# Attention, an MLP and a mixture of experts in one kernel: the next stage's first operands loaded and split elsewhere in attention's last iterations

## The chip, the cores and the metric

The kernel runs on one core of a Trainium2 chip. The core has a matmul engine (TensorE, PE in the profile, with its weight loads as PEld), a vector engine (VectorE, DVE), a scalar engine (ScalarE, ACT), GpSimd (POOL) and SyncE (SP), which here does nothing but issue DMAs. The profile counts 16 DMA engines that carry what SP and POOL issue. Each compute engine works its own instructions in order and waits at semaphores for the others. The metric is the device time in microseconds of one execution.

## The reference, cut to what matters

Three stages follow each other; all is float32.

```python
# attention, for B = 8 batches and H = 8 heads, S = 512 tokens, 32 state rows, D = 64
a     = softmax(x @ state.T * scale);   xread = a  @ state     # tokens read the state
a2    = softmax(state @ x.T * scale);   sread = a2 @ x         # the state reads the tokens
x     = concat([xread, sread]) -> rows of B*(512+32) tokens x 512
# an MLP over all 4352 rows
h = x @ w_in;  g = h - tanh(h);  x = g @ w_out
# one of 8 experts for each row
out[row] = gate[row] * (relu(x[row] @ w1[e]) @ w2[e])
```

## The kernel before

**Attention** (lines 418 to 759) takes 16 units, a unit being four heads of one batch: unit i is batch i // 2, half i % 2. A hand-written loop over t (line 704, t = 1 to 18) runs them as a pipeline: iteration t turns the tokens of unit t (`attn_x`), has the scores and both softmaxes of unit t-1, the reads of unit t-2, and in `attn_read_turn` turns the state's result xs of unit t-3 into xo, which goes to the scratch tensor `x_state_t` in DRAM. Beside it the loop makes sixteen pieces of state @ w_in (`sw_part`, t = 1 to 16), which go to the scratch tensor `state_w_in`, and the tokens' probabilities of each unit go to `probs_t`. The matmul that would form xread is not made: the next stage multiplies the probabilities with state @ w_in instead.

Stores are collected in `later`, and `flush` at the head of the next iteration issues them, each time as state_w_in, x_state_t, state_w_in, probs_t. Loads are issued in the iterations too: `attn_load` the tokens xc of unit t+1 (five buffers), `win_load` a piece of w_in. SP works this list strictly in order. Its DMAs use eight counters in turn, so that an issue also waits until the eighth one before it has landed.

**The MLP** (lines 780 to 1113) goes over steps i = 16 b + f, with batch b and slice f of the hidden width. `mm1(b, f)` is six matmuls hp from the split operands at (the probabilities, as ath and atl) and sw (state @ w_in, as swh and swl). Each operand is a sum of a rounded high part (ACT's copy) and a low part (DVE's subtraction), both made by `split` (line 363). `g_series` turns hp into g on ACT and DVE, `g_split` splits g (low part on POOL for b = 0), `mm2` multiplies with w_out. For b = 0 the parts of w_out are still being made: `dec_load` loads the raw words, `dec_bits` joins them on ACT and DVE, `dec_split` writes them into the tile w1t.

The first batch's operands are fetched inside attention's loop: `load_sw(0, 0)` (two loads, one for each four heads) and `load_at(0)` read the scratch tensors into the raw tiles swf and atf, which have one buffer each; `split_sw` and `split_at` split a half at a time. These calls are what the change moves. The load of swf for four heads is

```python
t = raw["sw"] = pm.tile([P, 2, NX], F32, tag="swf", name="swf", bufs=1)
for c in range(2):
    nc.sync.dma_start(t[:, c], swd[q, b // 4, 4 * c : 4 * c + 4, b % 4])
```

so its source is four blocks (heads) of 32 rows of 2 KB. The tile xo has two buffers: `tmp("xo", (P, 2, NS))`, and the third xo in a row waits until the first has been stored.

The order on PE, ACT, DVE and SP is that of the code in attention's loop; around the boundary to the MLP each engine follows its own list, shown below where it differs.

Of the kernel before, what the change touches and what calls it, by code (L numbers as in the profile page):

```python
# [57 lines left out]
def whole(  # L58
# [102 lines left out]
    class Decoder:  # L161
# [32 lines left out]
        def split(self, key, hi, lo):  # L194
            m = self.parts.pop(key)
            return [nc.scalar.copy(hi, m), rest(nc.gpsimd, lo, m, hi)]
# [170 lines left out]
    def load_at(b):  # L367
        if b < B:
            t, src = pm.tile([P, 2, S], F32, tag="atf", name="atf", bufs=1), atd[b]
        else:  # L370
            t, src = pm.tile([P, NPR, NW], F32, tag="atf", name="xsf", bufs=1), xsd
        raw["at"] = t
        nc.sync.dma_start(t, src)

    def split_at(b, half):
        t = raw["at"]
        if half == 0:
            shape = list(t.shape)
            at[b] = tuple(
                pw.tile(shape, F32R, tag=n, name=n, bufs=2) for n in ("ath", "atl")  # L380
            )
        n = t.shape[1] // 2
        c = slice(half * n, half * n + n)
        split(at[b][0][:, c], at[b][1][:, c], t[:, c])

    def load_sw(b, q):
        t = raw["sw"] = pm.tile([P, 2, NX], F32, tag="swf", name="swf", bufs=1)
        for c in range(2):
            nc.sync.dma_start(
                t[:, c],  # L390
                swd[q, b // 4, 4 * c : 4 * c + 4, b % 4],
            )

    def split_sw(b, q, c):
        if c == 0:
            sw[b, q] = tuple(
                pw.tile([P, 2, NX], F32R, tag=n, name=n, bufs=2) for n in ("swh", "swl")
            )
        h, l = sw[b, q]
        split(h[:, c], l[:, c], raw["sw"][:, c])  # L400
# [12 lines left out]
    def dec_bits(b, f):  # L413
        dec.absolute((b, f))
        dec.bits((b, f))


    with ExitStack() as pe:
# [4 lines left out]
        def tmp(name, shape=(P, R, P), dt=F32, bufs=2):  # L423
            return pa.tile(list(shape), dt, tag=name, name=name, bufs=bufs)
# [38 lines left out]
        def load_state():  # L463
            nc.sync.dma_start(
                z[:, 1 : G + 1], state.rearrange("b h n d -> (b h n) d").rearrange("(p g) d -> p g d", g=G)
            )
# [4 lines left out]
        def turn_state(o, j0):  # L471

            n = min(4, G // 2 + o - j0)
            pt = ps_m.tile([P, 4, P], F32, tag="m", name="pt_state")
            for j in range(n):
                g = 1 + 2 * (j0 + j) - o
                nc.tensor.transpose(pt[:, j, :], z[:, g : g + 2].rearrange("p g d -> p (g d)"), ident)
            for up in range(2):
                js = [j for j in range(n) if 0 <= 2 * (j0 + j) - o + up < G]
                if not js:  # L480
                    continue
                g = 2 * (j0 + js[0]) - o + up
                rows = slice(up * D, up * D + D)
                for m in range(NS // G):
                    dst = st_g[rows, :, :, m, g : g + 2 * len(js) - 1 : 2]
                    src = pt[rows, js[0] : js[-1] + 1].rearrange(
                        "p j (b h m) -> p h b m j", b=B, h=H
                    )[:, :, :, m]
                    (nc.vector.tensor_copy if up else nc.scalar.copy)(dst, src)

        def split_state(k):
            c = slice(2 * k, 2 * k + 2)
            nc.scalar.copy(sth[:, c], st[:, c])
            rest(nc.vector, stl[:, c], st[:, c], sth[:, c])
# [5 lines left out]
        def win_load(i):  # L500
            n, k = divmod(i, NPR)
            wdec.load(i, wi32[k * P : (k + 1) * P, 2 * n * NX : 2 * (n + 1) * NX])

        def win_split(i):
            win[i] = tmp("winh", (P, NX), F32R, 3), tmp("winl", (P, NX), F32R, 3)
            wdec.split(i, *win[i])
# [28 lines left out]
        def attn_load(i):  # L535
            b, c = units[i]
            xcs[i] = tmp("xc", (P, 4, R, D), F32, 5)
            nc.sync.dma_start(
                xcs[i], x[b, 4 * c : 4 * c + 4].rearrange("h (p r) d -> p h r d", r=R)
            )  # L540
# [119 lines left out]
        def attn_read_turn(i):  # L660
            b, c = units[i]
            pt = ps_m.tile([P, P], F32, tag="m", name="pt_r")
            nc.tensor.transpose(pt, xss.pop(i).rearrange("p o d -> p (o d)"), ident)
            pt = pt.rearrange("p (k h n) -> p k h n", h=2, n=NS)
            xo = tmp("xo", (P, 2, NS))
            for hh in range(2):
                rows = slice(hh * D, (hh + 1) * D)
                nc.vector.tensor_copy(xo[rows], pt[rows, :, hh])
            later.append((xsd[:, 2 * c : 2 * c + 2, b * NS : (b + 1) * NS], xo))

        NU = len(units)
        LEAD = 3

        def piece(t):

            return [when.index(t)] if t in when else []
# [3 lines left out]
        with tc.manual_schedule():  # L680
            load_state()
            for i in piece(1):
                win_load(i)
            attn_load(0)
            for i in piece(2):
                win_load(i)
            attn_load(1)
            for o, j in ((0, 0), (0, 4), (1, 0), (1, 4), (1, 8)):
                turn_state(o, j)
            attn_x(0)  # L690
            for i in piece(1):
                wdec.absolute(i)
                wdec.bits(i)
            split_state(0)
            for i in piece(1):
                win_split(i)
            for i in piece(3):
                win_load(i)
            for k in range(1, NPR):
                split_state(k)  # L700
            for i in piece(2):
                wdec.absolute(i)
                wdec.bits(i)
            for t in range(1, NU + LEAD):
                def at_(fn, lag, *args):
                    if 0 <= t - lag < NU:
                        fn(t - lag, *args)

                now = piece(t)
                flush()  # L710
                at_(attn_load, -1)
                for i in piece(t + 3):
                    win_load(i)
                at_(attn_scores, 1)
                at_(attn_state, 1)
                at_(attn_x, 0)
                at_(attn_turn, 2)
                for i in now:
                    sw_part(i, 0)
                for i in piece(t + 2):  # L720
                    wdec.absolute(i)
                at_(attn_read_turn, 3)
                at_(attn_turn_scores, 1)
                at_(attn_state_exp, 1)
                at_(attn_soft, 1)
                for i in piece(t + 1):
                    win_split(i)
                for i in now:
                    sw_part(i, 1)
                at_(attn_soft_exp, 1)  # L730
                at_(attn_probs, 2)
                at_(attn_read, 2)
                at_(attn_state_norm, 1)
                at_(attn_read_copy, 2)
                for i in piece(t + 2):
                    wdec.bits(i)
                at_(attn_norm, 1)
                if t == NU - 1:
                    load_sw(0, 0)
                    load_at(0)  # L740
                    for f in range(3):
                        dec_load(0, f)
                if t == NU:
                    split_sw(0, 0, 0)
                    split_at(0, 0)
                if t == NU + 1:
                    split_sw(0, 0, 1)
                    split_at(0, 1)
                    dec_bits(0, 0)
                    load_sw(0, 1)  # L750
                if t == 1:
                    nc.sync.dma_start(lists.rearrange("(p n) t -> p n t", p=P), unlisted)
                    nc.sync.dma_start(yd[NTOK : NTOK + 1], zero[0:1])
                    for b in range(B):
                        nc.sync.dma_start(
                            yd[b * SEQ + S : (b + 1) * SEQ],
                            zero[b % 4 * NS : (b % 4 + 1) * NS],
                        )
            flush()
# [20 lines left out]
    with ExitStack() as pe:  # L780
# [294 lines left out]
        with tc.manual_schedule(engines={EN.PE, EN.Activation, EN.DVE, EN.SP}):  # L1075
# [71 lines left out]
            at_ = along(ij[:, 0:E], rank, ALU.is_equal)  # L1147
            nbp = small("nbp", E)
            wzp, cep = (const.tile([P, E], F32, name=n) for n in ("wzp", "cep"))
            for n, (dst, src) in enumerate(((nbp, nb), (wzp, wz))):  # L1150
                t = square()
# [315 lines left out]
    with tc.manual_schedule(engines={EN.PE, EN.SP, EN.Activation, EN.DVE}):  # L1467
# [26 lines left out]
        t = keep("t", NSB)  # L1494
# [71 lines left out]
    n = nc.values_load(used[0:1, 0:1], min_val=NBLK, max_val=NSB)  # L1566
# [35 lines left out]
```

## Time and profile before

| | us |
|---|---|
| three runs | 1287.59, 1290.66, 1291.16 |
| their median | 1290.66 |
| the profiled execution | 1288.32 |
| its span, first to last instruction | 1286.1 |
| PE busy in the span | 1233.2 (96%) |
| attention | to about 127 |
| MLP | from about 130 to 782 |
| experts | the rest |

The profiled execution's own time is 2.2 us above its span. The times of the change's place are read as instants from the start of the span. In the timeline a row has the start, the duration of the group, the engine and line, and in brackets the idle time ahead of it with what ended it. Rows of SP (SPq) show when a DMA was issued, not when it landed.

### The profile page before, as it was taken

The numbers are of one execution on the slowest core, as the hardware profiler recorded it, in microseconds if no ns is written. First come the engines' busy times: TensorE is split into PE (matmuls) and PEld (weight loads), VectorE is DVE, ScalarE is ACT, GpSimd is POOL, SyncE is SP. The second block draws the span as 40 slices with busy tenths as digits, with TensorE's granted clock in tenths as the row PEclk, the third lists the DMA queues.
The fourth block names the chain that finished last, engine by engine and source line by source line (L and its number), as shares of the span: only waits on it lengthen the run. The fifth ranks groups of instructions, "written<-read, shape, count | busy, mean of one in ns | idle before, by whom it ended". The sixth has DMA issues, their size and how long they took to land. (4 is left out here: it accounts for less than half of the span.)

```text
span 1286.1 us, 22737 instructions
## 1 busy us (share of the span) xinstructions
PE 1233.2 (96%) x6759; PEld 974.1 (76%) x6759; DVE 887.3 (69%) x1515; ACT 857.3 (67%) x1587; POOL 276.6 (22%) x315
## 2 busy tenths in 40 slices
PE   7989788999999999999999999999999999999994
PEld 4555566777777878777787888788888888888883
DVE  7998899677666767576666557566767767576562
ACT  7988677767676767667676673566665657566551
POOL 3333355112010101001010122323232222221100
PEclk8999799999999999999999999999999999999997
DMA  8998642413222222312232471755587877735251
GB/s 263 335 344 276 204 145 82 147 57 125 83 98 72 77 75 57 113 57 93 82 97 85 134 255 40 247 172 174 199 319 266 281 258 260 283 128 193 75 194 35
DMA packets 90277, 208.33 MB, mean 162 GB/s; under 512 B 14162, under 2 KB 30549, under 8 KB 88354
## 3 DMA queue, kind: packets, MB, share of 16 engines
q1 hardware_dynamic: 75682, 162.33, 38.0%
q0 software_dynamic: 14464, 44.40, 9.8%
q8 instruction: 64, 1.05, 0.4%
q14 instruction: 67, 0.55, 0.2%
HBM read 315.42 MB, written 75.03 MB: 304 GB/s over the span
## 5 line engine op out<-in xcount | busy, mean ns | idle before, releaser
L209 DVE SCALAR_TENSOR_TENSOR gs<-gs,gu 128x512 f32<-128x512 f32 (+1 forms) x144 | 104.0, 722 | 180.1 <-ACT gs L207 180.0
L859 PE MATMUL y<-w1t,gl 128*128 128x512 f32 x544 | 217.4, 400 | 8.6 <-POOL gl L159 8.0
L859 PE MATMUL y<-w1t,gh 128*128 128x512 f32 x544 | 223.2, 410 | 1.6 <-ACT gh L848 1.6
L859 PE MATMUL y<-w,gh 128*128 128x512 f32 x544 | 214.9, 395 | 0.0
L1450 PE MATMUL o<-w2t,w 128*128 (+1 forms) x888 | 212.8, 395 | 1.4 <-DVE w2t L1367 1.2
L1423 PE MATMUL h<-w1t,w 128*128 (+1 forms) x888 | 212.3, 395 | 0.0
L1367 DVE TENSOR_TENSOR w2t<-w2raw,w2t 128x1024 f32 (+1 forms) x140 | 171.3, 1226 | 40.3 <-ACT w2t L1366 30.7
L1450 PEld LDWEIGHTS o<-w2t,w 128*128 128x128 f32 x888 | 163.9, 188 | 35.8 <-issue 1.6
L1423 PEld LDWEIGHTS h<-w1t,w 128*128 128x128 f32 x888 | 164.0, 188 | 33.6 <-DVE w L1264 0.4
L206 ACT ACTIVATE gu<-hp 128x512 f32<-128x512 f32 (+1 forms) x144 | 82.3, 571 | 157.9 <-PE hp L829 157.7
L1366 ACT CAST w2t<-w2raw 128x1024 f32 (+1 forms) x140 | 147.2, 1054 | 19.9 <-issue 7.7
L859 PEld LDWEIGHTS y<-w1t,gl 128*128 128x128 f32 x544 | 102.6, 189 | 39.8 <-POOL gl L159 14.5
L829 PE MATMUL hp<-ath,swh 128*128 128x512 f32 (+1 forms) x320 | 123.7, 387 | 3.2 <-ACT ath L364 2.8
L859 PEld LDWEIGHTS y<-w1t,gh 128*128 128x128 f32 x544 | 102.5, 188 | 30.8 <-issue 6.4
L829 PE MATMUL hp<-atl,swh 128*128 128x512 f32 (+1 forms) x320 | 120.7, 377 | 0.7 <-DVE atl L365 0.7
L829 PE MATMUL hp<-ath,swl 128*128 128x512 f32 (+1 forms) x320 | 119.4, 373 | 0.0
L859 PEld LDWEIGHTS y<-w,gh 128*128 128x128 f32 x544 | 103.0, 189 | 21.2
L1429 ACT ACTIVATE hs<-h 128x512 f32<-128x512 f32 x74 | 43.8, 598 | 103.6 <-PE h L1423 103.6
L841 ACT ACTIVATE gu<-gu,nlim 128x512 f32<-128x512 f32 (+1 forms) x144 | 100.5, 698 | 9.4 <-DVE gs L209 8.0
L207 ACT ACTIVATE gs<-gu,b 128x512 f32<-128x512 f32 (+1 forms) x144 | 101.0, 701 | 6.3
L1251 POOL DMA_INDIRECT out_dram<-os,idx x39 | 40.4, 1035 | 274.5 <-DVE os L1250 259.4
L210 DVE SCALAR_TENSOR_TENSOR gs<-gs,hp 128x512 f32<-128x512 f32 (+1 forms) x144 | 94.7, 657 | 4.9
(257 smaller groups left out, 1929.4 us busy)
## 6 DMA issues: line engine op xcount, KB each, us to landing
w1t<-w_parts SPq DMA_DIRECT2D x35, 4096.0 KB
w2raw<-in_moe_w_dram SPq DMA_DIRECT2D x140, 512.0 KB
w_parts<-w POOLq DMA_DIRECT2D x48, 512.0 KB, 4.8
mot<-in_moe_w_dram SPq DMA_DIRECT2D x72, 256.0 KB
state_w_in<-swst SPq DMA_DIRECT2D x32, 512.0 KB
swf<-state_w_in SPq DMA_DIRECT2D x64, 256.0 KB
words<-in_moe_w_in_dram SPq DMA_DIRECT2D x16, 512.0 KB
xc<-in_x_dram SPq DMA_DIRECT2D x16, 512.0 KB
```

The lines of the kernel that those rows point to most:

```text
L206: nc.scalar.activation(u, hp, AF.Square)
L207: nc.scalar.activation(s1, u, AF.Square, bias=b1)
L209: nc.vector.scalar_tensor_tensor(s1, s1, QD, u, op0=ALU.add, op1=ALU.mult)
L210: nc.vector.scalar_tensor_tensor(s1, s1, QC2, hp, op0=ALU.mult, op1=ALU.mult)
L829: nc.tensor.matmul(hp, a[:, c, o : o + P], m[:, c, :], start=(n == 0), stop=(n == 3 * chunks - 1))
L841: nc.scalar.activation(u, u, AF.Relu, bias=nlim, accum_out=over[:, n : n + 1])
L859: mm = nc.tensor.matmul(y, g, w[f], start=(f == 0 and n == 0), stop=(f == NF - 1 and n == 2))
L1366: hi = nc.scalar.copy(to[0](i * CH), t)
L1367: lo = nc.vector.tensor_tensor(to[1](SLOT + i * CH), t, to[1](i * CH).bitcast(F32), op=ALU.subtract)
L1423: mm = nc.tensor.matmul(h, a[:, k, :], part(w1t, o1, lo_ * SLOT + k * F2 + half * NX), start=(n == 0), stop=(n == 11),)
L1429: nc.scalar.activation(hs[:, half * NX : (half + 1) * NX], h, AF.Relu)
L1450: mm = nc.tensor.matmul(o, a[:, k, :], part(w2t, o2, lo_ * SLOT + k * DM), start=(n == 0), stop=(n == 23))
```

## The change

Iteration 13 (t == NU - 3) now issues the loads of swf and atf, in place of iteration 15; the loads of the raw w_out words stay in iteration 15. Iteration 16 makes all four splits, where it made two and iteration 17 the other two. The load of the next swf (`load_sw(0, 1)`) moves from the end of iteration 17 to the end of 16. The last unit's `attn_read_turn` moves from iteration 18 to 17, right behind its `attn_read_copy`.

```diff
                 for i in piece(t + 2):
                     wdec.absolute(i)
-                at_(attn_read_turn, 3)
+                if t < NU + 2:
+                    at_(attn_read_turn, 3)
                 at_(attn_turn_scores, 1)
...
                 at_(attn_read_copy, 2)
+                if t == NU + 1:
+                    attn_read_turn(NU - 1)
                 for i in piece(t + 2):
                     wdec.bits(i)
                 at_(attn_norm, 1)
-                if t == NU - 1:
+                if t == NU - 3:
                     load_sw(0, 0)
                     load_at(0)
+                if t == NU - 1:
                     for f in range(3):
                         dec_load(0, f)
                 if t == NU:
-                    split_sw(0, 0, 0)
-                    split_at(0, 0)
+                    for n in range(2):
+                        split_sw(0, 0, n)
+                    for n in range(2):
+                        split_at(0, n)
+                    load_sw(0, 1)
                 if t == NU + 1:
-                    split_sw(0, 0, 1)
-                    split_at(0, 1)
                     dec_bits(0, 0)
-                    load_sw(0, 1)
```

SP's list from the load of unit 14's tokens (iteration 13) to that of unit 15's tokens (iteration 14), before:

```order
L538 DMA xc<-in_x_dram 128x4x256
L174 DMA words<-in_moe_w_in_dram 128x1024
L454 DMA state_w_in<-swst 128x2x512
L454 DMA x_state_t<-xo 128x2x32
L454 DMA state_w_in<-swst 128x2x512
L454 DMA probs_t<-ato 128x512
L538 DMA xc<-in_x_dram 128x4x256
```

and with the change:

```order
L538 DMA xc<-in_x_dram 128x4x256
L174 DMA words<-in_moe_w_in_dram 128x1024
L389 DMA swf<-state_w_in 128x1x512 x2
L373 DMA atf<-probs_t 128x1024
L454 DMA state_w_in<-swst 128x2x512
L454 DMA x_state_t<-xo 128x2x32
L454 DMA state_w_in<-swst 128x2x512
L454 DMA probs_t<-ato 128x512
L538 DMA xc<-in_x_dram 128x4x256
```

The three loads (swf twice, atf) stand ahead of iteration 13's stores and of unit 15's tokens, which they followed by a whole iteration before.

SP's list from the flush at the head of iteration 17 on, before:

```order
L454 DMA state_w_in<-swst 128x2x512
L454 DMA x_state_t<-xo 128x2x32
L454 DMA state_w_in<-swst 128x2x512
L454 DMA probs_t<-ato 128x512
L389 DMA swf<-state_w_in 128x1x512 x2
L454 DMA x_state_t<-xo 128x2x32
L454 DMA probs_t<-ato 128x512
L454 DMA x_state_t<-xo 128x2x32
```

and with the change:

```order
L389 DMA swf<-state_w_in 128x1x512 x2
L454 DMA state_w_in<-swst 128x2x512
L454 DMA x_state_t<-xo 128x2x32
L454 DMA state_w_in<-swst 128x2x512
L454 DMA probs_t<-ato 128x512
L454 DMA x_state_t<-xo 128x2x32
L454 DMA probs_t<-ato 128x512
L454 DMA x_state_t<-xo 128x2x32
```

The second pair of swf loads, which waits on DVE for the raw tile's last reader, now stands ahead of iteration 16's four stores. The first x_state_t in each list is that of unit 13.

DVE's list from its last normalisation on, before (L209 and L210 are the first step of g_series):

```order
L365 TENSOR_TENSOR swl<-swf,swh 128x512
L365 TENSOR_TENSOR atl<-atf,ath 128x512
L640 COPY e2t<-pt_e 128x512
L668 COPY xo<-pt_r 64x64 x2
L656 TENSOR_SCALAR xs<-px,s_2165 128x128
L365 TENSOR_TENSOR swl<-swf,swh 128x512
L365 TENSOR_TENSOR atl<-atf,ath 128x512
L185 TENSOR_SCALAR dec_l<-words 128x512
L187 SCALAR_TENSOR_TENSOR dec_m<-dec_m,dec_l 128x512
L190 SCALAR_TENSOR_TENSOR dec_m<-words,dec_m 128x512
L668 COPY xo<-pt_r 64x64 x2
L209 SCALAR_TENSOR_TENSOR gs_2320<-gs_2320,gu 128x512
```

and with the change:

```order
L365 TENSOR_TENSOR swl<-swf,swh 128x512 x2
L365 TENSOR_TENSOR atl<-atf,ath 128x512 x2
L640 COPY e2t<-pt_e 128x512
L668 COPY xo<-pt_r 64x64 x2
L656 TENSOR_SCALAR xs<-px,s_2165 128x128
L668 COPY xo<-pt_r 64x64 x2
L185 TENSOR_SCALAR dec_l<-words 128x512
L187 SCALAR_TENSOR_TENSOR dec_m<-dec_m,dec_l 128x512
L190 SCALAR_TENSOR_TENSOR dec_m<-words,dec_m 128x512
L209 SCALAR_TENSOR_TENSOR gs_2320<-gs_2320,gu 128x512
```

All four low parts now stand together ahead of unit 15's e2t, and the last xo (unit 15's) stands ahead of the first decoding of w_out (L185 to L190) where it stood behind it.

## Rows read from the trace of the kernel before

**Rows 1.** The page: busy time, and the DMA line in 40 slices of 32 us.

```profile
PE 1233.2 (96%) x6759; PEld 974.1 (76%) x6759; DVE 887.3 (69%) x1515; ACT 857.3 (67%) x1587; POOL 276.6 (22%) x315
...
DMA  8998642413222222312232471755587877735251
```

**Rows 2.** Timeline of PE around attention's end; the bracket is idle time and releaser.

```profile
126.79 0.33 PE L663 MATMUL pt_r<-ident,xs 128*128 128x128 f32 x1
129.96 0.80 PE L829 MATMUL hp<-ath,swh 128*128 128x512 f32 x1 [2.83 <-ACT ath L364]
...
143.34 0.48 PE L859 MATMUL y<-w1t,gh 128*128 128x512 f32 x1
```

**Rows 3.** Timeline of ACT: the split of the first at, and of the next swf.

```profile
129.29 0.62 ACT L364 CAST ath<-atf 128x512 fp32r<-128x512 f32 x1 [1.40 <-DMA atf<-probs_t]
...
143.67 0.62 ACT L364 CAST swh<-swf 128x512 fp32r<-128x512 f32 x1 [0.41 <-DMA swf<-state_w_in]
```

**Rows 4.** Timeline of DVE from the first split to the first g_series.

```profile
128.75 0.69 DVE L365 TENSOR_TENSOR swl<-swf,swh 128x512 fp32r<-128x512 f32 x1
...
135.00 0.46 DVE L668 COPY xo<-pt_r 64x64 f32<-64x64 f32 x2 [3.77 <-DMA x_state_t<-xo]
...
136.96 0.42 DVE L185 TENSOR_SCALAR dec_l<-words 128x512 int32<-128x512 int32 x1
...
139.75 0.69 DVE L209 SCALAR_TENSOR_TENSOR gs<-gs,gu 128x512 f32<-128x512 f32 x1 [0.47 <-ACT gs L207]
```

**Rows 5.** Timeline of SP: start and length of issues, 86 to 137 us.

```profile
86.25 0.57 SPq L538 DMA_DIRECT2D xc<-in_x_dram  x1
...
103.34 0.56 SPq L174 DMA_DIRECT2D words<-in_moe_w_in_dram  x1
...
109.22 0.67 SPq L538 DMA_DIRECT2D xc<-in_x_dram  x1
...
116.49 1.23 SPq L389 DMA_DIRECT2D swf<-state_w_in  x2
...
120.91 0.50 SPq L454 DMA_DIRECT2D x_state_t<-xo  x1
...
123.97 0.36 SPq L454 DMA_DIRECT2D state_w_in<-swst  x1
128.32 0.33 SPq L454 DMA_DIRECT2D probs_t<-ato  x1
...
136.47 1.09 SPq L389 DMA_DIRECT2D swf<-state_w_in  x2
```

**Rows 6.** SP's waits, 118 to 136 us: total, times, longest.

```profile
SPq L454 <- DMA swf<-state_w_in: 6.4, 2, 3.9
```

**Rows 7.** Stretches: busy time of engines, then granted clock, DMA share, GB/s.

```profile
113.00:114.00 1.00, 1.00 (x40) 0.56 (x40) 0.90 (x2) 1.00 (x4) 0.24 (x1) 1.00 1.08 396
...
114.50:115.00 0.50, 0.50 (x9) 0.09 (x7) 0.50 (x3) 0.50 (x2) 0.50 (x1) 1.00 0.42 126
...
128.00:135.00 7.00, 4.24 (x40) 2.73 (x40) 2.70 (x5) 2.81 (x5) 0.00 (x0) 0.57 1.05 390
...
137.00:138.00 1.00, 0.90 (x2) 0.81 (x3) 0.90 (x3) 0.00 (x0) 0.00 (x0) 0.50 0.26 92
```

**Rows 8.** Timeline of PE: scores and token turns of iterations 12, 14, 15 and 16.

```profile
90.53 0.64 PE L563 MATMUL ps_s<-xT,st 64*32 64x256 f32 x8
...
93.69 1.06 PE L549 MATMUL pt_x<-ident,xc 128*128 128x128 f32 x8 [1.64 <-DMA xc<-in_x_dram]
...
106.60 0.64 PE L563 MATMUL ps_s<-xT,st 64*32 64x256 f32 x8
...
114.96 1.41 PE L549 MATMUL pt_x<-ident,xc 128*128 128x128 f32 x8
...
120.40 0.64 PE L563 MATMUL ps_s<-xT,st 64*32 64x256 f32 x8
```

## The prediction, made before the changed kernel was run

> **What bounds the kernel now.** I read the page first, then the boundary between attention and the MLP engine by engine, then SP's issues and the DMA share. PE is busy for 96% of the span [rows 1], so time can only be won where PE stands still or runs at the lower clock. The boundary is such a place: PE waits 2.83 us for the first high part of at, and between its last attention transpose at 126.79 and the first mm2 at 143.34 it does only two of mm1's rounds and attention's remains [rows 2]. ACT had waited for atf to land [rows 3], though SP issued it by 118.2, some 11 us earlier. DVE waited 3.77 us for a store of x_state_t that SP had issued at 120.91, 14 us before [rows 4, 5]. So DMA sets the boundary's pace: the share is 1.05 from 128 to 135 [rows 7]. The change goes at the right place. But the DMA line shows 8 to 9 tenths in attention too [rows 1]: the loads are moved into a queue that is full there as well.
>
> What a pair of swf loads does to that queue is the reader's main point. From 137 to 138 the DMA share is 0.26 at 92 GB/s, while 16 busy engines move 390 GB/s [rows 7]: about four of the sixteen still work, long after the others have nothing left. A load of swf reads four blocks of rows. If each block is one engine's, the pair puts 512 KB on four engines, 98 GB/s together, and whatever is issued behind it waits there while twelve engines run ahead. The 32 KB store that took 14 us from issue to its waiter is what that looks like [rows 4, 5]. The trace names no engines, so this is an inference from shares and latencies.
>
> The Trainium skill, "DMA: Bandwidth & Descriptors", section "Why a DMA increments its semaphore by 16 and not by 1", says that a transfer is spread over the largest number of engines up to 16 that divides the slowest dimension on both sides, and takes the lowest-numbered ones; with four heads slowest both loads would share the same four. By it the pair's price is the one on four engines, 5.4 us below; with all sixteen it would be 1.3 us, and the first term below would shrink to 2.8. The shares in rows 7 are what I rest on.
>
> **Term A: the loads in iteration 13.** They go out behind the words load of 103.34 and ahead of the tokens of unit 15, issued at 109.22 [rows 5] and first used by PE at 114.96 without a wait [rows 8]. How much margin had that load? The share is 1.08 from 113 to 114 and 0.42 from 114.5 to 115 [rows 7]: the queue ran dry just then, so I take 0.5 us. That attention lives near this edge is shown by iteration 12: tokens issued at 86.25 kept PE waiting 1.64 us until 93.69 [rows 5, 8].
>
> The added work ahead of it on the four engines: the pair, 512 KB at 98 GB/s, 5.4 us; atf, 512 KB over all sixteen at 390 GB/s, 1.3 us. Less the margin that is 6.2 us of PE's wait at pt_x in iteration 15. A wait costs more than itself, since the clock falls: from iteration 12's scores at 90.53 to iteration 14's at 106.60 are 16.07 us, and two undisturbed iterations take 120.40 - 106.60 = 13.80 [rows 8], so a wait of 1.64 cost 2.27, that is 0.63 more. A = 6.8 us.
>
> Bounds. From above, the pair beside other reads: SP, whose eighth issue back was a swf load, was held until 123.97 and 128.32 for the two loads [rows 5, 6], so the second came 4.35 us after the first; twice that is 8.7, and A = 8.7 + 1.3 - 0.5 + 0.6 = 10.1. From below, if the pair spread over all sixteen: 1 MB at 390 GB/s is 2.7, and A = 2.7 - 0.5 + 0.6 = 2.8; below that only zero, if later DMAs aren't queued behind earlier ones. I take the middle one, since beside the moved pair stand stores and tokens rather than the w_out loads that followed it before.
>
> **What goes away at the boundary.** With swf and atf in place, ACT's four copies follow each other and PE has its first operands some 2 us earlier; DVE makes the four low parts from 128.75 on, 4 times 0.69. Were nothing else late, DVE would reach the first g_series after its xo, xs, xo and the decoding. Between 135.00 and 139.75 that work took 4.75 us [rows 4], of which two low parts, 1.4, are now made before; started at 132.2 (after the four and e2t, 5 times 0.69) it would end at 135.6 to 137.3, the latter with the 1.7 or so that PE's lower clock may add to the turn of xs. That is a gain of 2.4 to 4.1, middle 3.2. mm1 alone gains more, but ACT's cast of w_out and everything behind it waits for DVE's decoding.
>
> **Term B: the last xo.** Something else is late. The last unit's xo now stands ahead of the decoding on DVE. Having two buffers, it waits for the store of unit 13's xo. In SP's list that store moved behind the second pair of swf loads, and that pair waits for DVE's second swl, ready at 128.75 + 2 x 0.69 = 130.1. The pair's issue takes 1.09 and two issues of about 0.4 follow, so the store is issued at about 132.0; ahead of it on the four engines stand the pair again and one state_w_in (512 KB over sixteen, 1.3). When does it land? From below, 130.1 + 5.4 + 1.3 = 136.8, as if data flowed at the instant of issue. From above: at 136.47 a pair was issued, and ACT waited for its first half until 143.67 [rows 3, 5], 7.2 us; a second half at 98 GB/s is 2.7, the store ahead 1.3: 130.1 + 11.2 = 141.3. I take 139.5, nearer to the upper one since that is a measured landing, though with w_out loads beside it. Then xo (0.46) and the decoding (136.96 to 138.9 or so, 1.95) bring the first g_series to 141.9, where it was at 139.75: B = +2.2, with ends -0.5 and +4.0. The wait of 3.77 is not removed but replaced by one behind the next pair. Queued behind it on DVE are the decoding and g_series, behind that ACT's cast of w1t, POOL's low part and mm2.
>
> The work itself is the same: no instruction is added or removed but waits; the splits and the turn cost what they did, so those edits get nothing. Moving four splits together puts two of them ahead of e2t, 1.4 us on DVE, which is contained in B's instants.
>
> **The sum.** A 6.8 + B 2.2 = +9.0 us. Both lie on the path: attention's iteration is a chain through PE, and after the boundary PE is never idle long enough to catch up. Against the profiled execution, 1288.32 + 9.0 = 1297.3. That execution is 2.3 us below the median of the runs shown, from which it would be 1299.7; I name the middle, 1298.5.
>
> **Rivals.** (1) *Faster.* If DMAs issued later are not held up behind the swf pair, there is neither A nor B, and the boundary's gain is left; its upper end of 4.1 then, since PE without waits keeps its clock where the granted one was 0.57 from 128 to 135 [rows 7]: 1286.6 from the median. For it: ACT and PE did wait for these loads. Against it: the 14 us of a 32 KB store. It decides at the point where unit 15's tokens land by 114.96 and unit 13's xo store by about 134. Chance 0.18. (2) *No change.* The pair is spread over more engines than I think: A 2.8, and B gives way to the gain of 3.2: about -0.4, 1290. Against it stands the share of 0.26. Chance 0.11. (3) *A without B.* Tokens late, but the xo store lands in time: 6.8 - 3.2 = +3.6, 1294. For it: the lower end of B is just below zero. Chance 0.12. (4) *B without A*: the margin of unit 15's tokens is larger than it looks: +2.2, 1293. Chance 0.06. My forecast, both, has 0.53, and its own range is 1294 to 1305 by the ends of A and B.
>
> **How the numbers follow.** A measurement of this kernel can tell about 0.3%, 3.9 us, from no change. Slower by more: nearly all of the forecast, 0.51, and a good third of rival 3, 0.05, so 0.56. Faster by more: rival 1 is at that line, and I give two thirds of it, 0.12. Between: the rest of rivals 1 and 3, rivals 2 and 4, and the forecast's lower end, 0.32. The range leaves out most of rival 1 and little above: 1289 to 1304.
>
> **What would show it.** Right: PE idle for 4 us or more in front of pt_x in iteration 15, released by the DMA of xc; the lower clock behind that; SP's issue of the second swf pair ahead of four stores; DVE idle at the second of the two last xo, released by x_state_t; no wait of ACT for atf. Wrong: pt_x of iteration 15 starts at 115 as before, or the last xo doesn't wait; then A or B falls, and the difference between the starts of the first mm2 says by how much. If the gap at the boundary shrinks and the whole is slower, the loss is in attention, and A is its size.

## The result, and the profile after

The changed kernel is slower: 1296.36 us (median of 9 runs, 1294.40 to 1298.18) against 1287.92 us for the kernel before (9 runs). The ratio is 1.0062 [1.0051 to 1.0073], that is 6.6 to 9.4 us more. The profiled execution took 1298.18 us with a span of 1296.3, the longest of its nine, so the instants below show a loss 1.4 us larger than the medians do (1298.18 - 1288.32 = 9.9, against 8.4).

The page of the changed kernel, to be read beside [rows 1]: busy time, then PE, its granted clock and the DMA share in 40 slices of 32 us.

```profile
PE 1231.3 (95%) x6759; PEld 973.6 (75%) x6759; DVE 888.6 (69%) x1515; ACT 857.9 (66%) x1587; POOL 276.8 (21%) x315
...
PE   6987688999999999999999999999999999999994
...
PEclk9998799999999999999999999999999999999998
DMA  7998353332322232222222382644587968745241
```

PE and its granted clock in the kernel before:

```profile
PE   7989788999999999999999999999999999999994
...
PEclk8999799999999999999999999999999999999997
```

PE's busy time is 1.9 us shorter while the span is 10.2 longer: nothing was added, PE waits. It waits more in the fourth and fifth slices (7 and 6 tenths busy where it was 9 and 7, clock 8 and 7 tenths where it was 9 and 7), from 97 to 162 us, which are the end of attention and the boundary. The timeline of PE there, beside [rows 2, 8]:

```profile
113.74 0.64 PE L563 MATMUL ps_s<-xT,st 64*32 64x256 f32 x8
...
122.55 1.94 PE L549 MATMUL pt_x<-ident,xc 128*128 128x128 f32 x8 [7.26 <-DMA xc<-in_x_dram]
...
134.43 0.66 PE L638 MATMUL pt_e<-ident,e 128*128 128x128 f32 x4
...
152.65 0.80 PE L833 MATMUL hp<-ath,swh 128*128 128x512 f32 x1 [7.85 <-DVE gs L210]
...
155.37 0.63 PE L863 MATMUL y<-w1t,gh 128*128 128x512 f32 x1
```

Two long gaps: 7.26 us ahead of pt_x of iteration 15, ended by the DMA of its tokens, where [rows 8] had none; and 7.85 us ahead of a round of mm1, ended by DVE. The first mm2 starts at 155.37, which is 12.03 later than in [rows 2]. Attention's last pt_e starts at 134.43, and at 126.10 before, so 8.3 us are lost in attention. Counted from the scores of the iteration with the wait (113.74, and 113.50 before), 8.1 of them lie behind those scores.

SP's issues say why the tokens came late, beside [rows 5]:

```profile
104.74 1.22 SPq L389 DMA_DIRECT2D swf<-state_w_in  x2
106.00 0.49 SPq L373 DMA_DIRECT2D atf<-probs_t  x1
106.60 0.59 SPq L454 DMA_DIRECT2D state_w_in<-swst  x1
107.29 0.93 SPq L454 DMA_DIRECT2D x_state_t<-xo  x1
108.31 1.08 SPq L454 DMA_DIRECT2D state_w_in<-swst  x1
109.49 1.85 SPq L454 DMA_DIRECT2D probs_t<-ato  x1
111.43 1.11 SPq L538 DMA_DIRECT2D xc<-in_x_dram  x1
...
138.96 1.09 SPq L389 DMA_DIRECT2D swf<-state_w_in  x2
...
140.62 0.57 SPq L454 DMA_DIRECT2D x_state_t<-xo  x1
```

The moved pair and atf stand behind the words load, as planned. Behind them each issue takes longer than the one before, up to 1.85 us for a store of probs_t, which takes 0.33 in [rows 5]; the tokens go out behind that one, at 111.43 where it was 109.22. Later the second pair goes out at 138.96, with four stores behind it.

The timeline of DVE, beside [rows 4], from the four low parts to the first g_series:

```profile
137.65 1.28 DVE L365 TENSOR_TENSOR swl<-swf,swh 128x512 fp32r<-128x512 f32 x2
138.85 1.28 DVE L365 TENSOR_TENSOR atl<-atf,ath 128x512 fp32r<-128x512 f32 x2
...
148.83 0.46 DVE L668 COPY xo<-pt_r 64x64 f32<-64x64 f32 x2 [5.49 <-DMA x_state_t<-xo]
...
151.19 0.68 DVE L209 SCALAR_TENSOR_TENSOR gs<-gs,gu 128x512 f32<-128x512 f32 x1
```

And that of ACT, beside [rows 3], with the split of at and the first cast of w1t:

```profile
137.20 1.14 ACT L364 CAST ath<-atf 128x512 fp32r<-128x512 f32 x2
...
151.34 0.62 ACT L196 CAST w1t<-dec_m 128x512 fp32r<-128x512 f32 x1 [8.47 <-DVE dec_m L190]
```

What the change was to remove is gone: ACT no longer waits for atf, and the four low parts follow each other on DVE from 137.65 to 140.1. In its place DVE waits 5.49 us for the store of unit 13's xo, and ACT's cast of w1t waits 8.47 us for DVE. The first g_series starts at 151.19 where it was 139.75: 11.4 later, of which 8.3 came from attention and 3.1 from the boundary.

The DMA share by stretches, beside [rows 7] (the columns are the same):

```profile
119.00:122.00 3.00, 0.00 (x0) 0.00 (x0) 0.00 (x0) 0.00 (x0) 0.40 (x1) 0.50 1.03 337
...
126.00:127.00 1.00, 1.00 (x8) 0.40 (x5) 0.07 (x1) 0.10 (x1) 0.00 (x0) 0.66 0.25 102
...
135.00:140.00 5.00, 1.68 (x9) 1.08 (x9) 4.67 (x12) 4.33 (x8) 0.00 (x0) 1.00 0.01 2
...
140.00:141.00 1.00, 1.00 (x5) 0.78 (x4) 0.99 (x4) 0.00 (x0) 0.00 (x0) 0.67 0.11 18
...
146.00:149.00 3.00, 0.00 (x0) 0.00 (x0) 0.17 (x1) 0.00 (x0) 0.00 (x0) 0.69 0.26 94
```

From 119 to 122 all compute engines but POOL stand still while the DMA share is 1.03. From 146 to 149 the share is again 0.26, as in [rows 7] behind a pair. And from 135 to 140 the queue carries almost nothing (2 GB/s): the pair of 138.96 met an empty queue, and still the store issued behind it at 140.62 ended DVE's wait only at 148.83.

### The profile page after: what moved, and what is told of

It reads as the page before. It is cut to its first block, busy times and chain, and to the rows that moved or that the text cites. A ratio compares the mean times of both kernels' runs of the same rounds, so it can differ in the third digit from the quotient of the medians.

```text
span 1296.3 us, 22733 instructions
## 1 busy us (share of the span) xinstructions
PE 1231.3 (95%) x6759; PEld 973.6 (75%) x6759; DVE 888.6 (69%) x1515; ACT 857.9 (66%) x1587; POOL 276.8 (21%) x315
## 5 line engine op out<-in xcount | busy, mean ns | idle before, releaser
L209 DVE SCALAR_TENSOR_TENSOR gs<-gs,gu 128x512 f32<-128x512 f32 (+1 forms) x144 | 104.0, 722 | 178.7 <-ACT gs L207 178.7
L210 DVE SCALAR_TENSOR_TENSOR gs<-gs,hp 128x512 f32<-128x512 f32 (+1 forms) x144 | 94.7, 657 | 4.9
```

Source lines behind the costliest of these rows:

```text
L209: nc.vector.scalar_tensor_tensor(s1, s1, QD, u, op0=ALU.add, op1=ALU.mult)
L210: nc.vector.scalar_tensor_tensor(s1, s1, QC2, hp, op0=ALU.mult, op1=ALU.mult)
```

## The experiments

Each edit but the last is against the changed kernel. Two instants carry most of the comparison: attention's last pt_e on PE, and DVE's first g_series (L209). Their distance is the length of the boundary. Each is a row of that kernel's timeline, in its one profiled execution; the ratio is to the kernel before, in the same comparison. An instant of one profile is good to a microsecond or so: in e1 attention ends 1.3 us earlier than before, though its edit leaves attention's work and loads up to that point as they were. The distance and the ratio are safer.

| kernel | last pt_e | first g_series | distance | ratio [95%] |
|---|---|---|---|---|
| before | 126.10 | 139.75 | 13.65 | |
| the change | 134.43 | 151.19 | 16.76 | 1.0062 [1.0051, 1.0073] |
| e1, loads back | 124.78 | 145.85 | 21.07 | 1.0055 [1.0040, 1.0071] |
| e2, next sw back | 133.35 | 146.04 | 12.69 | 1.0036 [1.0025, 1.0047] |
| e3, loads one earlier | 126.11 | 138.50 | 12.39 | 0.9985 [0.9974, 0.9995] |
| e4, first pair contiguous | 128.35 | 144.88 | 16.53 | 1.0052 [1.0036, 1.0068] |
| e5, both pairs contiguous | 131.97 | 144.67 | 12.70 | 1.0002 [0.9987, 1.0016] |
| e6, decoding earlier | 126.29 | 137.67 | 11.38 | 0.9980 [0.9966, 0.9995] |
| e7, the turn alone | 126.59 | 143.21 | 16.62 | 1.0030 [1.0012, 1.0048] |

### e1: the first loads back in iteration 15

```diff
-                if t == NU - 3:
+                if t == NU - 1:
                     load_sw(0, 0)
                     load_at(0)
```

> The change with its loads of swf and atf back in iteration 15; splits, next swf and turn stay as changed. Theory (a pair of swf loads queues on four engines; A is unit 15's tokens behind it, B the last xo behind the next pair): PE doesn't wait for xc in iteration 15, so A is gone, but the last xo waits for its store behind the w_out words and the next pair, until about 143, and the first g_series starts at 145 to 147, some 6 us later than before the change: ratio to before 1.002 to 1.006. Rival (the loads in iteration 13 are the whole loss, the rest of the change is a gain): no wait at the last xo over 2 us, first g_series before 139.75, ratio 0.997 to 1.000.

1296.83 us (4 runs). DVE at the boundary:

```profile
143.49 0.46 DVE L668 COPY xo<-pt_r 64x64 f32<-64x64 f32 x2 [7.72 <-DMA x_state_t<-xo]
...
145.85 0.68 DVE L209 SCALAR_TENSOR_TENSOR gs<-gs,gu 128x512 f32<-128x512 f32 x1
```

Attention is undisturbed, pt_x of iteration 15 starts without a wait for tokens, and A is gone. The wait for the xo store is still there, and longer: the boundary takes 7.4 us more than before (21.07 against 13.65), and the first g_series comes 6.1 later. So the early loads are not the whole loss. Not all of the 7.4 is the second pair's, for the first pair is back in iteration 15 as well, and the earlier turn makes the boundary 3.0 us longer without any load being moved (e7).

### e2: the second pair back at the end of iteration 17

```diff
-                    load_sw(0, 1)
                 if t == NU + 1:
                     dec_bits(0, 0)
+                    load_sw(0, 1)
```

> The change with only the next swf loads back at the end of iteration 17, behind the flush that stores unit 13's xo. Theory: the wait of 7 us for unit 15's tokens stays, the last xo waits under 1 us, the first g_series comes 4 to 5 us earlier than in the changed kernel (146 to 147): ratio to before 1.002 to 1.004. Rival (the wait of the last xo is caused by the crowded DMA queue in general, not by its place behind the next pair): the wait stays at 4 us or more and the ratio at 1.006.

1294.82 us (8 runs). PE's token turn in iteration 15:

```profile
121.33 1.94 PE L549 MATMUL pt_x<-ident,xc 128*128 128x128 f32 x8 [7.05 <-DMA xc<-in_x_dram]
```

SP's issues of unit 13's xo and of the second pair:

```profile
132.47 0.36 SPq L454 DMA_DIRECT2D x_state_t<-xo  x1
...
137.79 1.09 SPq L389 DMA_DIRECT2D swf<-state_w_in  x2
```

DVE's last xo and first g_series:

```profile
143.69 0.46 DVE L668 COPY xo<-pt_r 64x64 f32<-64x64 f32 x2 [0.90 <-PE pt_r L663]
...
146.04 0.68 DVE L209 SCALAR_TENSOR_TENSOR gs<-gs,gu 128x512 f32<-128x512 f32 x1
```

The mirror image: PE's wait for tokens stays (7.05 us), DVE's wait for the store goes, since SP now issues the four stores from 131.79 to 135.12 ahead of the pair at 137.79. The boundary is 1.0 us shorter than before, and attention 7.3 longer. Against the changed kernel only the place of the second pair differs, and it is worth 4.1 us of the boundary (16.76 to 12.69); the intervals of the two ratios don't meet.

### e3: the first loads one iteration earlier than before, not two

```diff
-                if t == NU - 3:
+                if t == NU - 2:
                     load_sw(0, 0)
                     load_at(0)
...
-                    load_sw(0, 1)
                 if t == NU + 1:
                     dec_bits(0, 0)
+                    load_sw(0, 1)
```

> The change with the loads in iteration 14, behind the issue of unit 15's tokens, and the next swf loads at the end of iteration 17: both causes undone, what is left of the idea kept. Theory: no wait for tokens over 1 us, swf and atf there before ACT wants them, no wait of DVE at either of the last two xo over 1.5 us, first g_series at 136 to 138: 2 to 4 us faster than before, ratio 0.997 to 0.9985. Rival (early loads hurt attention wherever they are put, since its DMA share is near one): a stall of 3 us or more in iterations 15 or 16 and a ratio over 1.000.

1288.43 us (12 runs) against 1290.27 (21 runs): faster, by 0.6 to 3.4 us. PE's token turn in iteration 15:

```profile
114.50 1.41 PE L549 MATMUL pt_x<-ident,xc 128*128 128x128 f32 x8
```

PE's first mm2:

```profile
142.36 0.50 PE L863 MATMUL y<-w1t,gh 128*128 128x512 f32 x1 [0.73 <-ACT gh L852]
```

DVE at the boundary:

```profile
135.18 0.35 DVE L656 TENSOR_SCALAR xs<-px,s 128x128 f32<-128x128 f32 x1 [2.31 <-PE px L649]
...
136.15 0.46 DVE L668 COPY xo<-pt_r 64x64 f32<-64x64 f32 x2 [0.62 <-PE pt_r L663]
...
138.50 0.68 DVE L209 SCALAR_TENSOR_TENSOR gs<-gs,gu 128x512 f32<-128x512 f32 x1
```

In iteration 14 the loads follow the tokens of unit 15 (issued at 108.76, the pair at 109.55), no later tokens exist to be delayed, and the boundary keeps its gain. The gain is small, 1.25 us at the first g_series, which was expected at 136 to 138 and came at 138.50: with no DMA late, DVE waits 2.31 us for PE's px, which PE has behind mm1's first matmuls. From e2 this kernel differs only in the iteration of the first loads; that is worth 7.2 us of attention, and the intervals of the ratios don't meet. So each of the two moved loads has a pair of kernels in which nothing else differs, e2 and e3 for the first loads, the change and e2 for the second.

### e4: the first pair from contiguous rows

```diff
-                swd[q, b // 4, 4 * c : 4 * c + 4, b % 4],
+                swd[q, b // 4, 4 * c : 4 * c + 4, b % 4] if (b, q) != (0, 0)
+                else swd[q, b // 4, 4 * c].rearrange("b r n -> (b r) n"),
```

> The change, but the first pair of swf loads reads, in place of four heads' rows of one batch, the rows of four batches of one head: the same bytes in 128 rows that lie one behind the other in DRAM (the first batch's first slice is computed from other rows). Theory (four blocks mean four engines): on sixteen engines the pair takes 1.3 us in place of 5.4 or more, PE's wait for unit 15's tokens falls from 7.3 to 1.5 to 3 us, the wait of the last xo stays (the next pair is as it was): ratio to before 1.002 to 1.004. Rival (it is the bytes, 1 MB more in a full queue, or SP's later issue): the wait for the tokens stays at 6 us or more, ratio 1.006.

1296.57 us (4 runs). PE's token turn in iteration 15:

```profile
116.94 1.06 PE L550 MATMUL pt_x<-ident,xc 128*128 128x128 f32 x8 [2.01 <-DMA xc<-in_x_dram]
```

SP's issue of those tokens:

```profile
109.36 0.37 SPq L539 DMA_DIRECT2D xc<-in_x_dram  x1
```

The pair now reads 128 rows in a run instead of four blocks of 32, other rows of the same scratch tensor, so the first batch's first slice is not the reference's; size, place in SP's list and work are the same. PE's wait falls from 7.26 to 2.01 us, and the tokens are issued at 109.36 again, since the issues ahead of them are short again (0.74 us at most from 105.63 on). Attention loses 2.3 us, not 8.3. The boundary, whose second pair is unchanged, is as long as in the changed kernel (16.53 against 16.76). The total came out above what was expected; its interval reaches into the expected one, and four runs don't settle it. Its profile has one more wait of PE for tokens, 1.97 us in iteration 11, ahead of anything that the edit moves.

### e5: both pairs from contiguous rows

```diff
-                swd[q, b // 4, 4 * c : 4 * c + 4, b % 4],
+                swd[q, b // 4, 4 * c : 4 * c + 4, b % 4] if b or q > 1
+                else swd[q, b // 4, 4 * c].rearrange("b r n -> (b r) n"),
```

> The change as it is, but both of the first two pairs of swf loads read the rows of four batches of one head, 128 rows one behind the other, in place of four heads' rows of one batch (the first two slices of the first batch are computed from other rows). Theory: with the second pair on sixteen engines too, the last xo waits under 2 us in place of 5.5, beside the tokens' wait that is already down to about 2; first g_series 2 to 4 us earlier than with the first pair alone (144.9), at 141 to 143: ratio to before 1.000 to 1.003. Rival (the last xo waits because SP issues its store so late, behind DVE's second swl, on whatever engines): the wait stays at 4 us or more, ratio 1.004 to 1.005.

1289.04 us against 1289.18 (10 and 29 runs): no difference. DVE at the boundary:

```profile
142.31 0.46 DVE L669 COPY xo<-pt_r 64x64 f32<-64x64 f32 x2 [0.92 <-PE pt_r L664]
```

In this order of SP's list, with the four stores still behind the second pair, the last xo no longer waits for a store, and the boundary falls from 16.53 (e4) to 12.70. The first g_series was expected at 141 to 143 and came at 144.67. The profiled execution was the longest of its ten, with waits for tokens in earlier iterations of attention too, so its last pt_e and all behind it come late; the distance and the ratio are what count. As in e4 the values are not the reference's, here in the first two slices of the first batch. With both pairs read in this shape the change costs nothing that can be measured (the interval reaches from 1.7 us faster to 2.1 slower).

### e6: e3, and the first decoding ahead of the turns

```diff
+                if t == NU + 1:
+                    dec_bits(0, 0)
                 at_(attn_read_copy, 2)
...
                 if t == NU + 1:
-                    dec_bits(0, 0)
+                    load_sw(0, 1)
```

(with the first loads in iteration 14 and the second pair in 17, as in e3)

> The kernel with the loads in iteration 14 and the next pair in iteration 17 (e3), and the first decoding of w_out put on DVE and ACT ahead of the last xs, where DVE waited 2.31 us for PE in that run. Theory (after the two waits are gone DVE's list sets the boundary): the decoding fills that wait, the first g_series moves from 138.5 to 136 to 137, first mm2 about 2 us earlier than 142.4: ratio to before 0.9965 to 0.998. Rival (PE or DMA sets the boundary by now): no earlier first mm2, ratio 0.998 to 0.999.

1286.60 us against 1289.18 (12 and 29 runs): faster than before by 0.6 to 4.4 us. DVE at the boundary:

```profile
133.07 0.43 DVE L185 TENSOR_SCALAR dec_l<-words 128x512 int32<-128x512 int32 x1
...
137.18 0.46 DVE L668 COPY xo<-pt_r 64x64 f32<-64x64 f32 x2 [1.29 <-PE pt_r L663]
137.67 0.69 DVE L209 SCALAR_TENSOR_TENSOR gs<-gs,gu 128x512 f32<-128x512 f32 x1
```

PE's first mm2:

```profile
141.75 0.63 PE L864 MATMUL y<-w1t,gh 128*128 128x512 f32 x1
```

The decoding now fills part of the time in which DVE waited for px. The first g_series comes 0.8 us earlier than in e3, where 1.5 to 2.5 was expected, because xo still stands ahead of it and waits for PE. The first mm2 comes only 0.6 us earlier, where 2 was expected: the ratio fell into the expected range, but DVE's list alone does not set the boundary. It beats both the kernel before and the change; against e3 the intervals overlap.

### e7: the kernel before with the last unit's turn moved, and nothing else

```diff
-                at_(attn_read_turn, 3)
+                if t < NU + 2:
+                    at_(attn_read_turn, 3)
...
                 at_(attn_read_copy, 2)
+                if t == NU + 1:
+                    attn_read_turn(NU - 1)
```

> The kernel before, with only the last unit's turn of xs moved to its own iteration. Theory (a last xo that stands earlier on DVE meets its store of unit 13 before that has landed, and holds the splits behind it): DVE waits 1.5 to 3 us at the last xo, the second low parts and the decoding come later by as much, first g_series at 142 to 143.5: ratio to before 1.0015 to 1.003. Rival (the turn is harmless, the loss came from the loads and the next pair): no wait at the last xo over 0.5 us, ratio 0.9990 to 1.001.

1293.85 us (10 runs): slower by 1.5 to 6.2 us. DVE at the boundary:

```profile
138.72 0.46 DVE L668 COPY xo<-pt_r 64x64 f32<-64x64 f32 x2 [2.35 <-DMA x_state_t<-xo]
...
143.21 0.69 DVE L209 SCALAR_TENSOR_TENSOR gs<-gs,gu 128x512 f32<-128x512 f32 x1 [0.84 <-ACT gs L207]
```

Moving the last xo ahead of the low parts and the decoding makes both wait for a store. The earlier turn pays only where that store has landed by then, as in e3. This store stands behind no pair that was just issued: in this run SP issues the first pair at 116.54, the store at 131.28 and the second pair only at 139.93. Yet from 136 to 139 the DMA share is 0.26 to 0.28 at 98 to 104 GB/s, as in [rows 7]. Engines that were held up by the first pair and are now behind with their shares of the later stores would look like that; the trace names no engines, so this is an inference too.

## Why the prediction was right, and where its sizes were off

The forecast was both terms, and both came. Against the profiled execution it gave 1297.3 us, and the profile of the changed kernel has 1298.18; the named 1298.5 is 2.1 above the median, within the range. Of the 2.1 us, 1.6 come from where the sum started, at 1289.5, where nine runs of the kernel before have a median of 1287.92. The forecast's own range has a slip: the ends of A and B, +2.3 and +14.1, give 1293 to 1305 from the median of the runs shown, not 1294.

That 9.0 lies so close to the 8.4 of the medians is partly luck. In the profile the two terms are 8.3 and 3.1, together 11.4 at the first g_series, 2.4 more than forecast. Two things hide that: the profiled executions differ by 1.4 us more than the medians do, and 1.2 us of the delay are regained behind the boundary, where the prediction had said that nothing would be.

**Term A, 6.8 predicted, 8.3 measured**, within its bounds of 2.8 and 10.1. The place, the releaser and the reason held. The term that was too small is the wait itself, 6.2 against 7.26. The working counted the data ahead of the tokens and took their issue as unmoved; in fact SP's own issues grew longer behind the pair, and the tokens were issued 2.2 us late. From issue to PE's start they took 11.12 us where it was 5.74, 5.4 more. In e4, with the same loads in the same place but no four blocks, the issues are short and the wait is 2.01, close to the 2.2 of the lower bound (2.7 less the margin of 0.5). The surcharge for the clock was about right: from pt_x to the last pt_e are 11.88 us (122.55 to 134.43) against 11.14 before, 0.7 for the 0.6 that was taken; the granted clock was 0.50, the lower level of 1.2 GHz, from 119 to 122 while PE stood.

**Term B, 2.2 predicted, 3.1 measured**, also within its ends. The store was taken to land 9.4 us after DVE's second swl (139.5 less 130.1). DVE was released 9.9 us after it: swl ended at 138.93, SP issued the pair at 138.96, and xo ran at 148.83. That is half of what B was short of; the other half is DVE, which ended its second swl 4.5 us behind the last pt_e (134.43 to 138.93) where 4.0 had been taken. The window rows show the part that the lower end left out: from the issue until 141 the queue moved hardly anything (2 and 18 GB/s). These 2 us, 5.4 for the pair and 1.3 for the state_w_in ahead of the store come to 8.7, or 147.7, an estimate 1.1 short of the xo (5.4 and 1.3 are the prediction's own terms). That the wait is one behind the pair is shown by e2 (stores ahead of the pair, no wait) and e5 (pair in another shape, no wait).

**The inference of four engines** was the step on which both terms stood. It is still an inference, for the trace names no engines, but it now has a test: with the source in a run of 128 rows instead of four blocks, PE's wait shrinks from 7.26 to 2.01 us and DVE's from 5.49 to none. By the rule of the Trainium skill, "DMA: Bandwidth & Descriptors", section "Why a DMA increments its semaphore by 16 and not by 1", four slowest blocks mean four engines and a run of 128 rows sixteen. These waits agree with that rule. e4 and e5 also change where in DRAM the rows lie, so a cause there is not excluded by them. A layout of state_w_in in which a batch's heads lie in a run, which would keep the computation, was not tried.

**What was over-sized is the gain at the boundary**, 2.4 to 4.1 with 3.2 in the middle. Where no DMA is late at the boundary, in e2, e3 and e5, the distance falls from 13.65 to 12.39 to 12.70, a gain of 1.0 to 1.3. The step that failed is that DVE's work, "started at 132.2", "would end at 135.6 to 137.3": it let DVE run on, while xs depends on PE's px, which in PE's list stands behind seven hp. In e3 DVE waits 2.31 us for it, and with attention ending at the same instant as before (126.11) the first g_series starts at 138.50. The 1.7 us put down to PE's lower clock at the turn of xs has no row behind it. Nor did PE have its first operands "some 2 us earlier": the first hp starts 3.86 us behind the last pt_e before, 3.83 with the change and 3.91 in e3, where ACT's second swh and PE's pt_a stand ahead of it. And between the last pt_r and the first mm2 PE does three rounds of mm1 in the kernel before (18 hp), not two; no term hangs on that. The sum was not touched by this error, since term B replaced the gain, but rivals 1 to 3 were given too short a time by some 2 to 3 us.

**The rivals.** Rival 1 (no wait behind the pair) fell with the first profile: tokens and store both late. Rival 2 (the pair spread) is what e5 makes of the change, and no difference came out, as worked out; but the interval is too wide to tell whether its terms were right, and the gain of 3.2 in it was too large. The change as it stands is not that case. Rival 3 (A without B) is e2, at about 4.6 us where 3.6 was worked out. Rival 4 (B without A) is nearest to e1, at about 7.1 where 2.2 was worked out; but e1 has the first pair back in iteration 15 too, which the rival had not. Taken one load at a time the loss splits so: the first loads in iteration 13 instead of 14 cost 0.0051 in the ratio (e3 to e2), the second pair an iteration early 0.0026 (e2 to the change), and e3 gains 0.0015 over the kernel before: 6.6 and 3.4 less 1.9 us, about 8.0. Of the 11.4 us at the first g_series the changed kernel has regained 1.2 by the end of the span, nearly all of it behind the MLP: the MLP's last mm2 starts at 793.08 and started at 781.82, still 11.3 later.

## What to carry to other kernels

Before a load is moved to an earlier place in a queue, read from the DMA share how many engines it keeps busy when it runs alone: a small share for a long time marks a load behind which later transfers can wait, however small (here a store of 32 KB, for 8.2 us). Move it behind the last transfer that the running stage needs (e3), or give its source another shape, and keep stores that free a buffer ahead of it (e2). When the waits for DMA are gone, look which instruction each engine would wait for next, before a gain is counted.

## What was not expected of the hardware

Behind the pair SP itself slowed down: five issues in a row took 0.59, 0.93, 1.08, 1.85 and 1.11 us, where issues of these DMAs take 0.33 to 0.67 in [rows 5]. With the pair's source in a run of rows they took 0.33 to 0.74 in the same place. So the pair's shape can delay not only the data behind it but their issue. It is not the only cause: in e3 the stores behind the same four-block pair, in iteration 14, take 0.33 to 0.37, in e5 a store takes 1.06 at 105.64, ahead of any pair, and in the kernel before an issue of tokens takes 1.89 at 37.22. What lengthens an issue was not isolated.

And a pair that met an empty queue (2 GB/s from 135 to 140) still held a store for 8.2 us, from 140.62 to 148.83, more than the 5.4 us that the pair's own data would take on four engines (the prediction's estimate, 512 KB at 98 GB/s, from [rows 7]). The late start (18 GB/s until 141) and the stores issued beside it, which would have shares on the same four engines, are what is left to explain it; the trace does not show which.
